# Gated linear attention with a convolved gate: one weight tile split without TensorE, the check counted earlier, the last store on ScalarE, a new order of all instructions

## The chip, the cores and the metric

The kernel runs on one core of one Trainium2 chip. The metric is the device time of one execution in microseconds; the time given for a kernel is the median of its runs.

## What is computed

The reference has two parts. The first is a linear attention with a forget gate for each channel, for 4 sequences of 768 tokens and 8 heads of 48 channels:

```python
f = 1.0 / (1.0 + np.exp(-f_logit))
for t in range(S):
    state = f[:, :, t, :, None] * state + np.einsum('bhd,bhe->bhde', k[:, :, t], v[:, :, t])
    y[:, :, t] = np.einsum('bhd,bhde->bhe', q[:, :, t], state)
```

The second part takes the heads side by side as `x` (768 x 384 for each sequence):

```python
h = np.maximum(x @ w_in, 0.0)                      # 384 -> 1024
conv_out[:, t] = sum over k of conv_w[k] * h[:, t + k - 1]
gate = 1.0 / (1.0 + np.exp(-conv_out))
return (h * gate @ w_out).astype(np.float32)       # 1024 -> 384
```

The three weights are 64-bit floats, read as pairs of 32-bit words.

## The kernel before

**Attention.** The loop runs over 24 steps: 4 sequences times 6 chunks of 128 tokens. For each step ScalarE makes the two gate factors `e` from the running sum of the gate's logarithms; VectorE multiplies them into the tile that holds k and q (L566, "the kq product"); TensorE makes the scores (L588), turns k over (L581), multiplies the masked scores with v (L608), updates the state (L616) and applies the state carried from before (L652). For the first nine steps the running sum is a matmul on TensorE (L551), for the rest a scan on VectorE (L558). ScalarE and VectorE copy the result as a rounded part and a rest into `xT` (L665, L667), and small transfers on SyncE's queue bring 16 rows of each into place (L675, "the gather").

**Gated product.** For half a sequence (384 tokens) and each of 8 blocks of 128 hidden units, the first product takes nine matmuls (L705: rounded and rest parts, three of the four combinations). ScalarE applies the relu (L715), ScalarE and VectorE the convolution (L721, L725), the gate (L729) and its product (L731). For each tile of 128 tokens the gated values are parted again into `gh` (L748, ScalarE) and `gl` (L752, VectorE); the second product is 16 matmuls with `gh` and 8 with `gl` (L761). The result is copied (L767) and stored (L771).

**Splitting the weights.** A 64-bit weight becomes a rounded float `hi` and a rest `lo`, in `split_f64`. There are seven tiles: three of `w_in` (1024 columns of `hi` each) and four of `w_out` (768). `CFG["ez"]` has a letter for each. Letter `d` takes four VectorE operations (mask L416, combine L419, mask L429, scale L444), one ScalarE copy (L435), and then "the join": for each half of the tile TensorE adds three products with a unit matrix in PSUM (L452 to L454) and ScalarE copies the sum out (L457). Letter `r` has no join: six VectorE operations (L414, L416, L419, L422, L425, L427) and one ScalarE copy (L424). Before, the letters are `dddrrrr`: all three tiles of `w_in` are joined on TensorE.

**The check at the end.** The fast path holds only for gates and weights inside a range. All `w_in` and `w_out` are read once more late in the program (L786 to L792) and a maximum kept for each piece; at the end VectorE turns these and the gates into a count (L803 to L805), one tiny matmul adds it up (L807), VectorE casts it (L808), every engine loads it into a register (L811), and a branch (L813) skips the slow path.

**The order.** `ORDER` is a list of all 1231 planned operations, and each engine and SyncE's queue take theirs in this order. A number with a point says which buffer of a ring is taken, a `v` that an operation which can run on ScalarE or VectorE runs on VectorE. Twelve of the operations are fillers, each a product of zeros (L381, `stir`, two matmuls in the records), that only keep TensorE busy. `LAST` names the one output tile whose store ScalarE issues instead of SyncE; before, it is tile 2 of the last sequence.

## Time and profile before

| | us |
|---|---|
| median of 3 runs | 303.0 (302.75, 303.0, 305.2) |
| the profiled execution's own time | 303.39 |
| its span, first to last instruction | 301.5 |
| TensorE busy (4319 matmuls) | 293.1 (97%) |
| VectorE busy | 255.3 (85%) |
| ScalarE busy | 241.8 (80%) |

The profiled execution is 0.4 us above the median, and 1.9 us of it lie outside the span. Matmuls are pipelined and overlap in the records, so a busy TensorE is not one at its peak; where it counts, the distance from the start of one instruction to the start of the next is read instead. VectorE's instructions, too, overlap the next one by a little under 0.1 us. Stretches differ: attention fills the first 220 us, the gated product begins at 42 us and is alone from 220 us on.

### The profile page before, as it was taken

The numbers are of one execution on the slowest core, as the hardware profiler recorded it, in microseconds if no ns is written. First come the engines' busy times: TensorE is split into PE (matmuls) and PEld (weight loads), VectorE is DVE, ScalarE is ACT, GpSimd is POOL, SyncE is SP. The second block draws the span as 40 slices with busy tenths as digits, with TensorE's granted clock in tenths as the row PEclk, the third lists the DMA queues.
The fourth block names the chain that finished last, engine by engine and source line by source line (L and its number), as shares of the span: only waits on it lengthen the run. The fifth ranks groups of instructions, "written<-read, shape, count | busy, mean of one in ns | idle before, by whom it ended". The sixth has DMA issues, their size and how long they took to land.

```text
span 301.5 us, 10053 instructions
## 1 busy us (share of the span) xinstructions
PE 293.1 (97%) x4319; PEld 276.4 (92%) x4319; DVE 255.3 (85%) x413; ACT 241.8 (80%) x482; POOL 2.8 (1%) x16
## 2 busy tenths in 40 slices
PE   8979999999999999999999999999999999999994
PEld 5767787998999999999999999999999999999993
DVE  3787999999999998999999997878985498499543
ACT  5677989999966899998979975876957797788541
POOL 3000000000000000000000000000000000000000
PEclk9999999999999999999999999999999999999998
DMA  6994998601460346622362444346040611313151
GB/s 211 395 362 138 332 331 306 183 2 30 130 253 0 99 145 218 187 74 72 102 215 60 167 164 121 101 137 201 21 145 14 191 51 47 96 54 97 71 175 58
DMA packets 19188, 43.38 MB, mean 144 GB/s; under 512 B 2732, under 2 KB 10052, under 8 KB 19140
## 3 DMA queue, kind: packets, MB, share of 16 engines
q1 hardware_dynamic: 18996, 42.50, 43.2%
q8 instruction: 35, 0.57, 0.8%
q10 hardware_dynamic: 144, 0.20, 0.2%
q14 instruction: 13, 0.11, 0.1%
HBM read 35.61 MB, written 4.72 MB: 134 GB/s over the span
## 4 chain that ended last, share of the span: by engine, by line
PE 88%; ACT 4%; DVE 3%; DMA 2%; issue 1%; SPq 0%; DVEq 0%; ACTq 0%
PE mm L761 33%; PE mm L705 33%; PE Y L608 4%; PE Y L616 4%; PE Y L652 4%; PE Y L581 3%; PE S L588 3%; DMA kq<-in_kq_dram 2%; PE mm L551 1%; PE mm L452 1%; DVE kq L566 1%; PE S L381 1%; ACT g L721 1%; ACT st L638 1%; ACT L729 0%
## 5 line engine op out<-in xcount | busy, mean ns | idle before, releaser
L705 PE MATMUL mm<-xT,wi 128*128 128x384 f32 x576 | 107.2, 340 | 0.1
L705 PEld LDWEIGHTS mm<-xT,wi 128*128 128x128 f32 x576 | 100.4, 188 | 1.1 <-ACT wi L457 0.2
L725 DVE SCALAR_TENSOR_TENSOR g<-hb,cw,g 128x384 f32<-128x384 f32 (+1 forms) x128 | 74.0, 614 | 8.1 <-ACT g L721 7.8
L761 PE MATMUL mm<-wo,gh 128*128 128x384 f32 x384 | 70.9, 337 | 0.0
L761 PEld LDWEIGHTS mm<-wo,gh 128*128 128x128 f32 x384 | 66.5, 188 | 0.3
L715 ACT ACTIVATE hb<-mm 128x384 f32<-128x384 f32 x64 | 31.3, 489 | 16.6 <-PE mm L705 16.2
L721 ACT ACTIVATE g<-hb,cw 128x384 f32<-128x384 f32 (+1 forms) x64 | 37.4, 613 | 2.2 <-DVE gl L752 2.1
L761 PE MATMUL mm<-wo,gl 128*128 128x384 f32 x192 | 37.1, 337 | 0.0
L752 DVE TENSOR_TENSOR gl<-g,gh 128x1024 fp32r<-128x1024 f32 (+2 forms) x28 | 29.5, 1067 | 8.1 <-ACT gh L748 7.1
L761 PEld LDWEIGHTS mm<-wo,gl 128*128 128x128 f32 x192 | 33.5, 188 | 0.1
L566 DVE TENSOR_TENSOR kq<-kq,e 128x1024 f32<-128x1024 f32 x24 | 29.1, 1214 | 4.6 <-DMA kq<-in_kq_dram 4.6
L731 DVE SCALAR_TENSOR_TENSOR g<-g,hb 128x768 f32<-128x768 f32 (+1 forms) x32 | 30.2, 956 | 3.0 <-ACT g L729 2.7
L748 ACT CAST gh<-g 128x1024 fp32r<-128x1024 f32 (+2 forms) x28 | 25.8, 933 | 7.8 <-PE mm L761 4.6
L729 ACT ACTIVATE g<-g 128x768 f32<-128x768 f32 (+1 forms) x32 | 26.5, 844 | 0.0
L608 PE MATMUL Y<-am,v 64*64 64x64 f32 (+1 forms) x768 | 24.0, 219 | 0.5 <-issue 0.5
L608 PEld LDWEIGHTS Y<-am,v 64*64 64x64 f32 (+1 forms) x768 | 19.0, 127 | 0.8 <-issue 0.8
L596 DVE COPY_PREDICATED am<-mask,S 128x512 f32<-128x512 uint8 x24 | 17.6, 734 | 1.8 <-PE S L588 1.8
L558 DVE TENSOR_TENSOR_SCAN fb<-runs,fb 128x512 f32<-128x512 f32 x15 | 18.0, 1214 | 0.0
L588 PE MATMUL S<-kq 48*64 48x64 f32 x768 | 16.8, 220 | 0.9 <-DVE kq L566 0.9
L667 DVE TENSOR_TENSOR xT<-Y,xT 112x512 fp32r<-112x512 f32 x24 | 16.3, 682 | 1.5 <-ACT xT L665 1.5
L616 PEld LDWEIGHTS Y<-v,kp 64*48 64x48 f32 (+1 forms) x704 | 13.7, 127 | 3.8 <-issue 2.7
L616 PE MATMUL Y<-v,kp 64*64 64x48 f32 (+1 forms) x704 | 16.2, 214 | 1.0 <-issue 1.0
(100 smaller groups left out, 349.5 us busy)
## 6 DMA issues: line engine op xcount, KB each, us to landing
kq<-in_kq_dram SPq DMA_DIRECT2D x24, 512.0 KB, 5.4
v<-in_v_dram SPq DMA_DIRECT2D x24, 192.0 KB, 4.4
out_dram<-ob SPq DMA_DIRECT2D x23, 192.0 KB, 2.2
fb<-in_f_logit_dram SPq DMA_DIRECT2D x15, 256.0 KB, 4.6
kq<-in_moe_w_in_dram SPq DMA_DIRECT2D x6, 512.0 KB, 4.1
kq<-in_moe_w_out_dram SPq DMA_DIRECT2D x6, 512.0 KB, 4.0
xT<-xT SPq DMA_DIRECT2D x48, 48.0 KB, 4.2
xT<-in_moe_w_in_dram SPq DMA_DIRECT2D x4, 512.0 KB, 7.2
```

The costliest lines, as they stand in the source:

```text
L566: ox = plan.op("DVE", 1222, lambda e, X=X, E=E: nc.vector.tensor_tensor(buf(X), buf(X), buf(E), ALU.mult), ka, need=[o2, ld_x], use=[X, E])
L588: o = nc.tensor.matmul(scores()[t, j, p, :], buf(X)[r, 0, p, t], buf(X)[r, 1, p, t], start=True, stop=True)
L608: o = nc.tensor.matmul(out_of(Y, p, j, w, z), buf(V).rearrange("p h d -> p (h d)")[t, h * D:h * D + w], buf(AM)[t, j, p, :], start=x == 1 ...
L616: nc.tensor.matmul(pk(z)[HP * j:HP * j + w, p, :], buf(KP)[t, p, HP * j:HP * j + w], buf(V)[t, 2 * p + j, :], start=True, stop=True)
L705: nc.tensor.matmul(buf(ph)[:, :HS], wi[:, t, wl, f * P:(f + 1) * P], x_view(pl, u)[:, t, xl, :], start=(i == 0), stop=(i == 3 * KT - 1))
L715: nc.scalar.activation(hb[:, 2:HS + 2], buf(ph)[:, :HS], AF.Relu, scale=0.5)
L721: o = pl.op("ACT", 620, lambda e, cv=cv, hb=hb, n=n, f=f: nc.scalar.activation(cv(), hb[:, 1:n + 1], AF.Copy, scale=cw[:, 1, f:f + 1]), ke ...
L725: o = pl.op("DVE", 617, lambda e, cv=cv, hb=hb, n=n, f=f, w=w, sh=sh: nc.vector.scalar_tensor_tensor(cv(), hb[:, sh:n + sh], cw[:, w, f:f ...
L729: o = pl.op("ACT", 846, lambda e, cv=cv: nc.scalar.activation(cv(), cv(), AF.Tanh), key, need=last, use=[("g", u)], mode="T")
L731: gates[u, fp] = pl.op("DVE", 960, lambda e, cv=cv, fp=fp, n=n: nc.vector.scalar_tensor_tensor(cv(), cv(), 1.0, h_b[:, fp:fp + 2, 1:n + 1] ...
L752: los.append(pl.op("DVE", 150 + 134 * nn * NF // 128, lambda e, hv=hv, lv=lv, src=src: nc.vector.tensor_tensor(lv(), src(), hv().bitcast(F ...
L761: nc.tensor.matmul(buf(po)[:, :DM], view(g)[:, f, :], wo[:, f, wl, :], start=(i == 0), stop=(i == 3 * NF - 1))
```

## The change

Four edits, and a new `ORDER` in which every operation has a new place.

1. The third letter of `ez` becomes `r`: one of the three `w_in` tiles is split without the join, so five of the seven tiles are.
2. The count is planned like any other operation and put before the `gl` part of the last tile; the copy of the last tile waits for it.
3. `LAST` is now the very last tile: its store is issued by ScalarE.
4. Two loads change shape: the gates of the last two groups of three steps come in one transfer of 768 KB each instead of three of 256 KB, and the kq tile of step 20 comes in two halves.

```diff
-           ... m2d=48.268, ez='dddrrrr')
+           ... m2d=48.268, ez='ddrrrrr')
 ORDER = """
-91.0 92 93 143.0 161.1 45.0 94 100.1 96 144.0 7.1 162.1 97.1 23.1 95.0 10.0 24 145.0 4.0 146.0 8.1 179.2 147 5.0 98
+89.0 43.0 90 137.0 91 138.0 92 23.1 93.0 24 44.0 8.1 98.1 94 155.1 6.0 156.1 1.0 9.1 139.0 2.0 140.0 7.1 95.0 173.2
...
-    LAST = (B - 1, CPH - 1)
+    LAST = (B - 1, NC - 1)
...
+        once = g >= len(groups) - 2 and not turned
-        for i in range(m):
-            n = first[g] + i
+        for i in range(0, m, m if once else 1):
+            n, k = first[g] + i, m if once else 1
...
-        ld_x = plan.op("SP", 430, lambda e, X=X, b=b, c=c: nc.sync.dma_start(buf(X), kq_in[b, c]), (n, "kq"),
-                       take=[("kq", X)], size=512)
+        ld_x = [plan.op("SP", 430, lambda e, X=X, b=b, c=c, z=z: nc.sync.dma_start(buf(X)[:, z], kq_in[b, c][:, z]), (n, "kq"),
+                        take=[] if z.start else [("kq", X)], use=[X] if z.start else [], size=512 // k)
+                for k in (2 if n == N - 4 else 1,) for z in (slice(y * 2 // k, (y + 1) * 2 // k) for y in range(k))]
...
-                    nc.scalar.copy if e == "ACT" else nc.vector.tensor_copy)(buf(ob), buf(po)[:, :DM]), key, need=[o],
+                    nc.scalar.copy if e == "ACT" else nc.vector.tensor_copy)(buf(ob), buf(po)[:, :DM]), key, need=[o] + (extra if (b, m) == (B - 1, NC - 1) else []),
...
+    def counting(e):
+        a = nc.vector.tensor_scalar(ok[:, :n_ft], ft_all.rearrange("p b c n -> p (b c n)"), F_MIN, None, ALU.is_ge)
+        nc.vector.tensor_scalar(ok[:, n_ft:], far, HALF * HALF, None, ALU.is_lt)
+        return a, nc.vector.tensor_reduce(oks, ok, mybir.AxisListType.X, ALU.add)
+
+    o = plan.op("DVE", 620, counting, N + 3.9, need=checks + keeps)
+    o = plan.op("PE", 60, lambda e: nc.tensor.matmul(one(), oks, ones, start=True, stop=True), N + 3.91, need=[o], take=[("S", "pn")],
+                mode="t", n=4)
+    counted = plan.op("DVE", 140, lambda e: nc.vector.tensor_copy(cnt_i, one()), N + 3.92, need=[o], use=["pn"])
+    moe(plan, gathered, [counted])
```

**The start of SyncE's queue.** The first transfers before; `fb` is a gate tile, `kq` and `v` are tiles of a step, `xT` is here the buffer into which raw weights are loaded.

```order
L514 DMA fb_111<-in_f_token_dram 128x384 x3
L540 DMA kq_113<-in_kq_dram 128x1024
L540 DMA kq_114<-in_kq_dram 128x1024
L464 DMA xT_144<-in_moe_conv_w_dram 24x256
L514 DMA fb_112<-in_f_token_dram 128x384
L542 DMA v_117<-in_v_dram 128x384
L542 DMA v_118<-in_v_dram 128x384
L464 DMA xT_153<-in_moe_w_in_dram 128x1024 x2
L540 DMA kq_115<-in_kq_dram 128x1024
```

The same place in the changed kernel.

```order
L515 DMA fb_111<-in_f_token_dram 128x384
L464 DMA xT_143<-in_moe_conv_w_dram 24x256
L515 DMA fb_111<-in_f_token_dram 128x384
L544 DMA kq_113<-in_kq_dram 128x1024
L515 DMA fb_111<-in_f_token_dram 128x384
L547 DMA v_117<-in_v_dram 128x384
L464 DMA xT_150<-in_moe_w_in_dram 128x1024 x2
L515 DMA fb_112<-in_f_token_dram 128x384
L544 DMA kq_114<-in_kq_dram 128x1024
```

The first weight tile has moved ahead of the second step's kq tile; 2328 KB are on the queue up to its end, where it was 3224 KB.

**VectorE ahead of the sixth kq product.** Before, the rows from the second `w_in` tile's second mask on; `gh`, `gl` and `ob` are here work tiles of a split, `am` the masked scores, `sh` and `st` the state.

```order
L429 TENSOR_SCALAR gl_487<-gh_385 128x1024
L444 SCALAR_TENSOR_TENSOR ob_507<-xT_262,gl_487 128x1024
L667 TENSOR_TENSOR xT_305<-Y_109,xT_305 112x4x128
L596 COPY_PREDICATED am_89<-mask_86,S 128x512
L692 MEMSET hb 128x2x2
L566 TENSOR_TENSOR kq_116<-kq_116,e_121 128x1024
L566 TENSOR_TENSOR kq_114<-kq_114,e_122 128x1024
```

In the changed kernel, from the last operation of the second tile on, which is the one split by letter `r`.

```order
L427 SCALAR_TENSOR_TENSOR wi<-gl_406,gh_375 128x2x512
L602 COPY_PREDICATED am_89<-mask_86,S 128x512
L414 TENSOR_SCALAR gl_522<-g_323 128x768
L673 TENSOR_TENSOR xT_321<-Y_109,xT_321 112x4x128
L572 TENSOR_TENSOR kq_116<-kq_116,e_122 128x1024
L416 TENSOR_SCALAR gh_562<-g_323 128x768
L635 TENSOR_TENSOR sh_96<-Y_110,st_94 112x192
L419 SCALAR_TENSOR_TENSOR gh_562<-g_323,gh_562 128x768
L422 SCALAR_TENSOR_TENSOR gl_522<-gl_522,g_323 128x768
L638 TENSOR_TENSOR st_93<-Y_110,sh_96 112x192
L602 COPY_PREDICATED am_90<-mask_86,S 128x512
L572 TENSOR_TENSOR kq_114<-kq_114,e_121 128x1024
```

The fifth and sixth kq products stood side by side; now four operations of a `w_out` tile, one masked copy and two of the state lie between them.

**The end of SyncE's queue.** Before: the last two stores, then the count's load (TENSOR_LOAD) and the branch.

```order
L771 DMA out_dram<-ob_4032 128x384
L771 DMA out_dram<-ob_4079 128x384
L811 TENSOR_LOAD cnt_i
L811 ISA x2
L813 COMPARE_AND_BRANCH
```

Now:

```order
L777 DMA out_dram<-ob_4037 128x384
L822 TENSOR_LOAD cnt_i
L822 ISA x2
L777 DMA out_dram<-ob_4079 128x384
L824 COMPARE_AND_BRANCH
```

The count's load has moved ahead of the last store but one, and the last store (tile `ob_4083`) has left this queue for ScalarE's.

## Rows read from the trace of the kernel before

**Rows 1.** Busy time by stretch: PE, PEld, DVE, ACT, POOL, then PEclk, DMA share, GB/s.

```profile
8.44:32.66 24.22, 21.69 (x483) 17.12 (x482) 20.33 (x34) 18.17 (x46) 0.00 (x0) 1.00 0.84 305
32.66:42.28 9.62, 9.62 (x243) 7.72 (x244) 9.62 (x18) 8.78 (x25) 0.00 (x0) 1.00 0.97 310
42.28:72.00 29.72, 29.65 (x598) 26.93 (x598) 29.46 (x49) 29.25 (x61) 0.00 (x0) 1.00 0.48 161
72.00:130.00 58.00, 58.00 (x818) 56.13 (x820) 56.68 (x87) 51.54 (x95) 0.00 (x0) 1.00 0.43 138
130.00:220.00 90.00, 89.67 (x1730) 86.23 (x1718) 82.05 (x135) 74.97 (x158) 0.00 (x0) 1.00 0.39 122
220.00:297.20 77.20, 77.20 (x448) 76.91 (x443) 53.84 (x84) 54.22 (x95) 0.00 (x0) 1.00 0.30 93
```

**Rows 2.** The chain that ended last, in order of time: start, length, what.

```profile
11.89 0.43 PE S L381 x2
...
42.28 3.15 PE mm L705 x18
...
272.19 24.97 PE mm L761 x144
297.19 0.56 DVE ob L767
```

**Rows 3.** Timeline of TensorE, two joins and what follows them: start, length, instruction.

```profile
48.06 1.13 PE L452 MATMUL mm<-gh,ident 128*128 128x512 f32 x2
...
50.81 0.60 PE L581 MATMUL Y<-ident,kq 128*128 128x128 f32 x4
```

**Rows 4.** Groups by line, shapes apart: the split's operations; busy us, mean ns.

```profile
L457 ACT CAST wi<-mm 128x512 fp32r<-128x512 f32 x6 | 3.5, 604 | 0.0
...
L419 DVE SCALAR_TENSOR_TENSOR gh<-xT,gh 128x1024 int32<-128x1024 int32 x2 | 2.4, 1217 | 0.0
L444 DVE SCALAR_TENSOR_TENSOR ob<-xT,gl 128x1024 fp32r<-128x1024 uint32 x2 | 2.4, 1215 | 0.0
...
L416 DVE TENSOR_SCALAR gh<-xT 128x1024 int32<-128x1024 int32 x2 | 1.4, 679 | 0.0
```

**Rows 5.** Timeline, the first 20 us: first weight load, first kq product, first split.

```profile
5.88 1.30 SPq L464 DMA_DIRECT2D xT<-in_moe_w_in_dram  x2
...
8.44 1.23 DVE L566 TENSOR_TENSOR kq<-kq,e 128x1024 f32<-128x1024 f32 x1 [4.61 <-DMA kq<-in_kq_dram]
...
14.76 0.68 DVE L416 TENSOR_SCALAR gh<-xT 128x1024 int32<-128x1024 int32 x1
```

**Rows 6.** Timeline, 31 to 47 us: kq products five and six, sixth score, last scale.

```profile
31.53 2.35 DVE L566 TENSOR_TENSOR kq<-kq,e 128x1024 f32<-128x1024 f32 x2
...
39.38 0.68 PE L588 MATMUL S<-kq 48*64 48x64 f32 x32
...
45.52 1.21 DVE L444 SCALAR_TENSOR_TENSOR ob<-g,gl 128x1024 fp32r<-128x1024 uint32 x1
```

**Rows 7.** Timeline, the first tile of the second product, around 95 us.

```profile
94.90 1.28 DVE L752 TENSOR_TENSOR gl<-g,gh 128x1016 fp32r<-128x1016 f32 x2
...
97.27 1.03 PE L761 MATMUL mm<-wo,gl 128*128 128x384 f32 x5
```

**Rows 8.** Waits of TensorE's weight loads between 32.7 and 297 us: total, times, longest.

```profile
PEld Y L652 <- issue: 2.1, 10, 0.4
```

**Rows 9.** Lines L771, L811, L813, L979: ns min/median/max, first and last start.

```profile
297.77 0.34 SPq L771 DMA_DIRECT2D out_dram<-ob  x1
...
DMA to landing us min/median/max: 1.8/1.9/3.4
...
L811 SPq TENSOR_LOAD <-cnt_i x1: 539/539/539, 298.2 to 298.2; - x1
...
L813 SPq EVENT_SEMAPHORE  x8: 17/17/17, 299.6 to 300.2; - x8
...
L979 SPq EVENT_SEMAPHORE  x10: 17/28/28, 300.2 to 301.5; - x10
```

## The prediction

> **What bounds the kernel now.** I read the busy time by stretch first, because the share over the whole run mixes stages with different limits. From 32.66 us on TensorE is busy all the time, in every stretch up to 297.2 us [rows 1]. Ahead of that it is not: between 8.44 and 32.66 us TensorE lacks 2.5 us, VectorE 3.9 and ScalarE 6.1 of 24.22 us. The second thing in these rows is that TensorE is not alone. VectorE is full from 32.66 to 42.28 us, lacks 0.3 of 29.72 us after that and 1.3 of 58 us up to 130 us; only from 130 us on does it have room (82.05 of 90 us, then 53.84 of 77.2). ScalarE is full from 42 to 72 us.

> The chain that ended last comes next [rows 2]. Its last long piece is the second product, 24.97 us from 272.19 us on without a gap, and after it only the copy of the last tile. So a microsecond of TensorE's work that is taken out is a microsecond off the end, provided the other two engines can keep up where they are full as well. That proviso is the whole question here.

> **What the change takes from TensorE.** One tile of three loses its join, that is two join halves. Two of them stand side by side at 48 us [rows 3]: from the start of the first to the start of what follows is 50.81 - 48.06 = 2.75 us. Counted with the order: four halves stood ahead of the first product before and two do now, and two stand behind it in both. So 2.75 us go, all from the part ahead of 42.28 us, where the first product starts [rows 2]. One filler moves from the start to behind the last product: 0.43 us more [rows 2], between nothing (it stood in a gap) and 0.43; I take 0.4. Behind the last product it runs while the last tile is copied and stored.

> The new order changes how often TensorE goes over from one kind of work to another: 99 changes after against 94 before, counted in the order over products, scores, small attention matmuls and turns. No row shows the price of one change; the nearest is the wait of "issue" ahead of the carried-state matmuls, 2.1 us in ten [rows 8], 0.2 each. Five more cost between nothing and 1.0 us; I take 0.3, since that wait is only one of the kinds, and three more of the changes went away with the joins.

> **What it adds to VectorE.** On tiles of 1024 a mask takes 0.68 us and a combining or scaling operation 1.22 [rows 4]. Letter `d` has two of each, 3.8 us; letter `r` has three of each, 5.7 us. VectorE gets 1.9 us more. ScalarE loses the two copies of the join, 2 x 0.60 = 1.2 us [rows 4].

> The sixth kq product is the place to test it, because the sixth score stands behind it and the first product behind that. Ahead of it VectorE's list is now longer by the 1.9 us, by the first four operations of a `w_out` tile (two masks and two others on 768 columns, three quarters of the sum above, 2.8 us), and by a masked copy and a few short state operations (about 1.2): 5.9 us in all. Before, the sixth kq product began at 32.7 us (the second of the two, [rows 6]), and the score that needs it at 39.38 [rows 6]. So there were 39.38 - 33.88 = 5.5 us of slack. If VectorE keeps all its 3.9 us of idle time, the product ends at 33.9 + 5.9 = 39.8 us, and the score can start 0.4 us later than it did. If it gives all of it back, it ends at 35.9 us, and TensorE, 3.2 us earlier at 36.2 us, does not wait.

> Does the idle time go? Most of it lay between the first kq product at 8.44 and the first split at 14.76 us [rows 5], where VectorE waited for scores and had no weights to work on. The transfers come in the order of SyncE's queue, and the first weight tile now ends 2328 instead of 3224 KB down the queue. At 305 GB/s, the mean of that stretch [rows 1], 0.9 MB are 2.9 us. The second kq tile comes later by about as much, but VectorE has the split to do in that time. I take it that 2.5 us or more come back, which is what the first product needs to start 3 us earlier.

> Behind that, VectorE's work up to the tiles of the second product is nearly what it was: the `w_out` operations that came earlier are missing later, and three copies of k that VectorE made stand on ScalarE now. The first tile of the second product is the tightest place: its `gl` is ready at 96.2 us and used at 97.27 [rows 7], so TensorE may come 1.1 us sooner for nothing, and for the rest VectorE must be earlier too, by the same regained time.

> **What it changes at the end.** Before, the last copy starts at 297.19 us [rows 2], SyncE issues the store at 297.77 and then loads the count (0.54 us from 298.2), branches, and goes through eight waits from 299.6 to 300.2 us [rows 9]. By the median of its line the store has landed at 297.77 + 1.9 = 299.7 us. So SyncE's own path, not the store, set the end. Now the count is loaded ahead of the last store but one, and ScalarE issues the last store. SyncE then has only to wait for it; SyncE's transfers take eight semaphores in turn, and in the new order this one is the eighth, the last to be waited for. It ends at 299.7 instead of 300.2: 0.5 us, between nothing (ScalarE issues later, the landing takes up to 3.4) and 0.5. I take 0.4. The count itself costs TensorE a tiny matmul that it had before.

> The 768 KB gate transfers and the halved kq tile cost nothing in my sum: they serve steps for which VectorE has room (after 130 us), and the kq half only lets the wait start sooner. If a buffer came free late for a whole group, the group's first step would wait; the rows give no price for that, and I leave it to the range.

> **The sum.** 303.39 - 2.75 - 0.4 + 0.3 - 0.4 = 300.1 us for the profiled execution. The median was 303.0, 0.4 us below that execution, so 299.7 us. A measurement of this kernel can tell about 1% from no change, that is 3.0 us; the forecast lies just at that edge.

> **The rivals.** *VectorE keeps its idle time.* Then the sixth score starts at 39.8 instead of 39.38 us, the join halves and the filler that no longer stand ahead of it give TensorE nothing but waiting, and only the tail is left: 303.0 + 0.4 - 0.4 = 303.0 us. For it speaks that the second kq tile now stands behind 1.4 MB more on the queue; against it, the weights that come sooner.

> *VectorE sets the pace from 42 to 130 us.* It lacks only 1.6 of 87.7 us there [rows 1]; the 1.9 us of the new letter then go onto the end, with 0.4 back at the tail: 304.5 us. Against it stands that the work up to the second product is nearly the same in sum. [...]

> *Slower: the third `w_in` tile comes late.* The order keeps its join on TensorE right behind the first two blocks of the first product, and its second half is loaded only behind the first gather. Before, the last scale ended at 46.73 us [rows 6] and the join began at 48.06. Everything on TensorE stands behind this join, so each microsecond by which the scale ends after 46.8 us is one at the end. It must end 3.5 us later, at 50.3 us, for the whole to be 1% slower; at 51 us the time would be 303.0 + 4.2 - 0.4 = 306.8 us. VectorE's list up to there is only 0.5 us longer, which speaks against it.

> *More than forecast.* If the regained time on VectorE also removes the waits of TensorE ahead of 32.66 us, up to 2.5 us [rows 1], 1.8 of them would give 297.9 us.

> **Chances.** Forecast 0.58 (its own range 298.4 to 301.2), more 0.10, idle time kept 0.16, VectorE's pace 0.10, slower 0.06. Of the forecast's share three fifths lie below 300.0 us, 0.35; with the better case 0.45 for faster by over 1%. The rest of it with the two cases near 303 us makes 0.49 within 1%; slower is 0.06. The range goes from 297.8 to 303.2 us: it leaves out the slower case, most of the case of VectorE's pace and a little at the lower end.

> **What would show it.** Right: four join halves instead of six; the first product begins at 39 to 40 us; VectorE busy for more than 22 us between the first kq product and 32.7 us, with its first split at about 12 us; no wait of TensorE at the first tile of the second product; from the last matmul to the end 3.9 us instead of 4.3. Wrong: a first product at 42 us (idle time kept), waits of TensorE for `gl` or for a relu between 42 and 130 us (VectorE's pace), or a join that waits for its scale (the late tile).

## The result, and the profile after

The changed kernel takes 305.19 us (median of 21 runs, 304.4 to 310.9), the kernel before, run beside it on the same chip, 303.11 us (median of 21, 301.99 to 305.2). The ratio is 1.0067 with a 95% interval of 1.0047 to 1.0087: slower by 0.7%. The forecast was 299.7 us with a range of 297.8 to 303.2; the time lies outside it, on the other side of no change. The run of 310.9 us belongs to a slower state (mean granted clock 0.989), and the ratio leaves such runs out. The profiled execution of the changed kernel took 304.6 us with a span of 302.8; before, these were 303.39 and 301.5.

The busy time by stretch of the changed kernel (columns as in [rows 1], which are the same stretches of before):

```profile
8.44:32.66 24.22, 20.57 (x476) 16.04 (x475) 21.48 (x39) 19.09 (x50) 0.00 (x0) 1.00 0.83 314
32.66:42.28 9.62, 8.30 (x243) 7.40 (x243) 9.48 (x15) 8.17 (x22) 0.00 (x0) 1.00 0.75 223
42.28:72.00 29.72, 29.27 (x565) 26.52 (x564) 27.97 (x46) 28.33 (x56) 0.00 (x0) 1.00 0.59 199
72.00:130.00 58.00, 58.00 (x812) 56.02 (x811) 57.30 (x88) 50.46 (x97) 0.00 (x0) 1.00 0.41 124
130.00:220.00 90.00, 90.00 (x1718) 86.02 (x1720) 80.56 (x129) 78.64 (x170) 0.00 (x0) 1.00 0.41 128
220.00:297.20 77.20, 77.20 (x487) 76.67 (x482) 54.11 (x85) 53.37 (x94) 0.00 (x0) 1.00 0.27 87
```

From 42.28 us to the end of the second product TensorE is as full as before: 0.4 us less up to 72 us, 0.3 more from 130 to 220 us. The difference in idle time lies ahead of it: in the first two stretches TensorE is without work for 24.22 - 20.57 + 9.62 - 8.30 = 4.97 us, where it was 2.53 [rows 1]. That is 2.44 us more, and the joins that went are worth nearly as much (2.75). This is a timeline of TensorE at the third `w_in` tile's join, which stayed:

```profile
48.71 1.13 PE L452 MATMUL mm<-gh,ident 128*128 128x512 f32 x2
...
50.13 1.02 PE L452 MATMUL mm<-gh,ident 128*128 128x512 f32 x2
...
51.45 0.60 PE L587 MATMUL Y<-ident,kq 128*128 128x128 f32 x4
```

From 48.71 to 51.45 us it takes 2.74 us, as it did [rows 3], and there is one such pair fewer ahead of it. The chain that ended last (start, length, what) says where the gain stood afterwards:

```profile
42.22 3.19 PE mm L711 x18
...
272.86 22.19 PE mm L767 x128
...
298.22 0.56 DVE ob L773
```

The first product starts at 42.22 us, where it was 42.28 [rows 2]: nothing is left of the 2.75 us. The last copy starts at 298.22 us, where it was 297.19 [rows 2], so another 1.09 us were lost behind the start of the first product. Such places are those of one execution each: `e8` below has the same instructions up to the end, and its first product starts at 41.09 us.

What TensorE waited for, 0 to 66 us (what waited and for whom, us in total, times, longest), first before, then in the changed kernel:

```profile
PE mm L381 <- DVE stir L308: 1.2, 1, 1.2
PE Y L616 <- issue: 1.0, 1, 1.0
PE S L588 <- DVE kq L566: 0.9, 2, 0.5
PE S L381 <- DVE am L596: 0.3, 1, 0.3
PE mm L452 <- ACT wi L457: 0.3, 1, 0.3
PE Y L608 <- issue: 0.2, 1, 0.2
```

```profile
PE Y L614 <- issue: 1.8, 2, 1.4
PE mm L381 <- DVE stir L308: 1.2, 1, 1.2
PE Y L622 <- ACT kp L598: 1.0, 1, 1.0
PE mm L556 <- ACT e L567: 0.9, 2, 0.7
PE mm L556 <- issue: 0.6, 1, 0.6
PE Y L658 <- DVE st L638: 0.6, 1, 0.6
PE Y L622 <- issue: 0.3, 1, 0.3
```

The waits for ScalarE and VectorE changed their names (kq, am and wi before, kp, e and st after) and grew by about 1 us, from 1.5 to 2.5. The larger part is the one without a name: "issue", a wait in which nothing that the profile shows held the engine, grew from 1.2 to 2.7 us. The timeline shows the odd thing about it: three of the four places (TensorE's matmuls, in brackets the idle time before them).

```profile
30.59 0.34 PE L614 MATMUL Y<-am,v 64*48 64x64 f32 x8 [1.36 <-issue]
...
41.17 1.05 PE L556 MATMUL mm<-tri,fg 128*128 128x128 f32 x7 [0.62 <-issue]
...
47.68 0.37 PE L614 MATMUL Y<-am,v 64*64 64x64 f32 x10 [0.44 <-issue]
```

Each stands in the middle of matmuls of one line, with the same inputs as the matmul before it. I counted TensorE's instructions in the traces of all kernels here: weight loads, matmuls and the semaphore instructions between them, the first as number 0. Up to 66 us the stops of matmuls without a name (over 0.15 us) come at the 449th, 705th, 961st, 1217th, 1473rd and 1729th, and at no other; behind that the kernel before has one at the 4801st (0.33 us, at 137.45 us) and the changed kernel none. All are multiples of 256 apart. And of the queue that the profile calls "q8 instruction" one packet of 16 KB ends 1.2 to 1.6 us ahead of the stop's end, each time. This is its row of the DMA view of the changed kernel from 0 to 50 us:

```profile
q8 instruction: 6, 0.10, 0.8%
```

When each piece began, and in brackets how long TensorE had stood still for it (us; the last two rows are experiments, below):

```
piece's first instruction   449th        705th        961st        1217th   1473rd       1729th
before                      18.00 (0.96) 24.40 (0.17) 29.01        37.04    40.40        46.87
changed                     19.33        24.37 (0.29) 30.59 (1.36) 36.70    41.17 (0.62) 47.68 (0.44)
changed, thin weights       20.14        24.89        30.01 (0.27) 36.12    40.67 (0.69) 46.46
before, thin weights        19.91        26.17        30.81        38.83    42.20        48.64
```

Why there: these are the rates of the DMA engines in 40 slices from 14 to 35 us, before and after.

```profile
GB/s 424 387 412 432 366 383 389 407 404 358 408 381 399 416 328 103 70 35 0 0 0 31 0 140 133 421 311 145 243 240 331 360 395 386 372 363 391 380 365 363
```

```profile
GB/s 429 421 398 387 396 284 59 137 213 351 384 382 383 307 357 412 359 390 386 414 369 410 420 439 401 429 402 354 120 29 0 0 0 0 31 0 0 82 82 102
```

Before, the engines are nearly empty from 22 to 26 us (0 to 103 GB/s), and the packet of the 961st starts at 25.5 us. In the changed kernel they are full from 19 to 28.5 us (307 to 439 GB/s), and the same packet starts at 28.2. In both, TensorE had come to the piece before at 24.4 us. Up to 48 us in the two traces a piece's packet starts 0 to 4.2 us after TensorE has come to the piece before; behind that, where the engines move less [rows 1], from 3.2 us ahead of it to 2.9 us after it.

### The profile page after: what moved, and what is told of

Same layout as the page of the kernel before. It is cut to its first block, busy times and chain, and to the rows that moved or that the text cites. A ratio compares the mean times of both kernels' runs of the same rounds, so it can differ in the third digit from the quotient of the medians.

```text
span 302.8 us, 10039 instructions
## 1 busy us (share of the span) xinstructions
PE 291.9 (96%) x4311; PEld 274.7 (91%) x4311; DVE 254.2 (84%) x410; ACT 241.9 (80%) x489; POOL 2.8 (1%) x16
## 4 chain that ended last, share of the span: by engine, by line
PE 92%; DVE 3%; issue 2%; ACT 2%; DVEq 0%
PE mm L711 34%; PE mm L767 34%; PE S L594 4%; PE Y L614 4%; PE Y L658 4%; PE Y L622 3%; PE Y L587 3%; PE mm L381 2%; PE mm L556 2%; PE mm L452 1%; DVE kq L572 1%; DVE gh L419 1%; PE S L381 0%; ACT e L565 0%; DVE gh L416 0%
## 5 line engine op out<-in xcount | busy, mean ns | idle before, releaser
L711 PE MATMUL mm<-xT,wi 128*128 128x384 f32 x576 | 108.8, 341 | 0.0
L614 PE MATMUL Y<-am,v 64*48 64x64 f32 (+1 forms) x768 | 24.0, 220 | 1.8 <-issue 1.8
L644 ACT ACTIVATE st<-st,ft_all 112x48 f32<-112x48 f32 x72 | 18.1, 325 | 3.4 <-DVE st L638 3.3
L598 ACT COPY kp<-Y 128x512 f32<-128x512 f32 x24 | 13.9, 580 | 4.7 <-PE Y L587 4.6
L773 ACT COPY ob<-mm 128x384 f32<-128x384 f32 x22 | 10.3, 468 | 9.1 <-PE mm L767 9.0
```

What stands on the lines that cost most here:

```text
L614: o = nc.tensor.matmul(out_of(Y, p, j, w, z), buf(V).rearrange("p h d -> p (h d)")[t, h * D:h * D + w], buf(AM)[t, j, p, :], start=x == 1 ...
L711: nc.tensor.matmul(buf(ph)[:, :HS], wi[:, t, wl, f * P:(f + 1) * P], x_view(pl, u)[:, t, xl, :], start=(i == 0), stop=(i == 3 * KT - 1))
```

## The experiments

Two theories. F: the late pieces, behind the weight transfers, took the gain of the joins. The rival: VectorE's longer list, or the waits for ScalarE, hold TensorE, and a late piece only shows a wait that would come elsewhere.

**The letter alone, in the old order.** The third letter changes; on VectorE's list the two operations that it adds and three of a `w_out` tile get new places, the rest stays as before. `e6` spreads these operations differently over the list.

```diff
-           ... ez='dddrrrr')
+           ... ez='ddrrrrr')
...
```

> The kernel before with the letter r for the third tile and nothing else: its two join halves and their copies leave the old order, its two added VectorE operations stand behind the sixth kq product, the first three operations of the first w_out tile behind the masked copy that followed them. Theory A (the removed joins are worth their time; the new order gave it back in waits of TensorE ahead of 52 us): the two join halves are 2.75 us of TensorE, up to 1 us is lost to waits, 300.4 to 301.5 us beside 303.1. Rival B (VectorE sets the pace up to 130 us, so its 1.9 us more go onto the end): 303.1 to 305.0 us.

> The kernel before with the letter r once more, VectorE's list laid out with care: the fifth kq product ahead of the sixth, then the tile's two late operations, masked copy and state, and only behind them the w_out tile, whose second half stands behind the third w_in tile's. Theory A (the time of e1 came of its list: TensorE waited 1.7 and 2.9 us for VectorE where the joins had been, and the granted clock fell behind it): first product at 40.5 to 41.5 us, clock 1.0 throughout, 301.3 to 302.5 us beside 303.1. Rival B (VectorE's 1.9 us set the first product whatever the list): first product at 42.3 us or later, 303.0 to 305.0 us.

305.84 us, 1.0080 [1.0059, 1.0102], and 306.51, 1.0116 [1.0069, 1.0162]: slower both times, and above the ranges of both theories. In the profiled execution of `e1` (308.0 us, the longest of its eight) TensorE waits for VectorE (idle time in brackets), and the granted clock (the first of the last three columns of the second view) is then about half of full speed, 0.52:

```profile
33.91 0.66 PE L581 MATMUL Y<-ident,kq 128*128 128x128 f32 x4 [1.65 <-DVE kq L566]
...
40.28 0.70 PE L652 MATMUL Y<-kq,sh 48*48 48x64 f32 x16 [2.87 <-DVE st L632]
```

```profile
39.50:46.50 7.00, 6.22 (x141) 6.10 (x141) 6.97 (x11) 4.24 (x11) 0.00 (x0) 0.52 0.93 306
```

In `e6` the longest such wait is 2.6 us, and the granted clock is 1.00 around it. So in neither list did VectorE take the letter's 1.9 us without TensorE waiting for it; a new order was needed for the letter, as far as these two lists show.

**The letter back, in the new order.** The other half of that question: the old letter in the changed kernel, its two join halves put among the attention matmuls (the order's lines are left out here).

```diff
-           ... ez='ddrrrrr')
+           ... ez='dddrrrr')
...
```

> The changed kernel with the letter d for the third tile again: its two join halves stand in the new order behind the two running sums that follow the fourth score and the fifth turn, two VectorE operations go (1.9 us), the other five keep their places. Theory A (the removed work stood beside waits of TensorE ahead of the first product, so that taking it out bought little): the two halves cost less than 1 us, 304.3 to 306.0 us beside 305.2. Rival (in the new order TensorE's work there counts in full): 305.2 + 2.75 us, 307.2 to 308.3 us.

308.06 us, 1.0157 [1.0119, 1.0195]. So in the new order the letter gains 308.06 - 305.19 = 2.9 us, near the 2.75 of the sum (the two intervals leave more than 1 us either way); and the order with the other edits costs 308.06 - 303.11 = 5.0 us. (The place of the joins is my choice, the waits of "issue" in its profiled execution are 0.9, 1.4 and 1.5 us, and the granted clock falls there, to 0.58 from 44 to 46 us and 0.57 from 46 to 48, so neither is an exact price.)

**The last store.** ScalarE issues the last store in the old kernel (`e7`); SyncE issues it in the new one (`e8`).

```diff
-    LAST = (B - 1, CPH - 1)
+    LAST = (B - 1, NC - 1)
```

> The kernel before with the last store issued by ScalarE and nothing else. By the step of the prediction (SyncE's own path set the end, so its relief is worth 0.3 to 0.5 us): 302.6 to 302.8 us beside 303.1. Theory C (the store issued by ScalarE lands later and is the last to be waited for): 303.1 to 303.9 us.

> The changed kernel with the last store issued by SyncE again and nothing else (the store of the tile that LAST named before goes to ScalarE). Theory C (landing of the ScalarE store, 2.6 us in the profiled execution where SyncE's take 1.9, sets the end): 304.4 to 304.8 us beside 305.2. By the step of the prediction SyncE is late again: 305.2 to 305.7 us.

303.45 us, 0.9993 [0.9965, 1.0022], and 304.86 us, 1.0051 [1.0029, 1.0073]: no effect that these runs can tell in either kernel.

**The sixth kq product earlier.** VectorE's list of the changed kernel with the sixth kq product ahead of three operations of a `w_out` tile.

```diff
-L416 TENSOR_SCALAR gh<-g 128x768
-L419 SCALAR_TENSOR_TENSOR gh<-g,gh 128x768
-L422 SCALAR_TENSOR_TENSOR gl<-gl,g 128x768
 L638 TENSOR_TENSOR st<-Y,sh 112x192
 L572 TENSOR_TENSOR kq<-kq,e 128x1024
+L416 TENSOR_SCALAR gh<-g 128x768
+L419 SCALAR_TENSOR_TENSOR gh<-g,gh 128x768
+L422 SCALAR_TENSOR_TENSOR gl<-gl,g 128x768
```

> The changed kernel with the sixth kq product, and the state operations and the masked copy that go with it, ahead of three operations of the w_out tile on VectorE. Theory A1 (VectorE's longer list ahead of the sixth kq product is what holds the first product at 42.2 us): the product starts at 41.0 to 41.6 us and the time is 304.0 to 304.6 us beside 305.2. Rival A2 (TensorE's waits ahead of it, those without a releaser above all, hold it): 305.0 to 305.4 us.

306.1 us, 1.0095 [1.0069, 1.0121]. The wait for VectorE is gone, one of 1.0 us for ScalarE's copy of a join (L457) has come, the first product still starts at 41.88 us (A1 expected 41.0 to 41.6), and the piece of the 1729th stops TensorE for 2.36 us, after which the granted clock falls to 0.53:

```profile
49.61 0.37 PE L614 MATMUL Y<-am,v 64*64 64x64 f32 x10 [2.36 <-issue]
```

```profile
50.50:53.50 3.00, 3.00 (x17) 1.69 (x10) 3.00 (x6) 2.40 (x4) 0.00 (x0) 0.53 0.93 338
```

So VectorE's list alone is not what holds it.

**Weight transfers moved.** (F's expectations are called A2 in `e3`.) `e3` moves the first half of the third `w_in` tile three transfers back; `e13` puts both halves side by side ahead of the gathers; `e11` does the opposite in the kernel before, and loads both halves and a piece of `w_out` sooner, into its gap at 22 to 26 us.

```diff
-L464 DMA xT<-in_moe_w_in_dram 128x1024
 L547 DMA v<-in_v_dram 128x384
-L681 DMA xT<-xT 16x768 x2
 L544 DMA kq<-in_kq_dram 128x1024
-L681 DMA xT<-xT 16x768 x4
-L464 DMA xT<-in_moe_w_in_dram 128x1024
+L464 DMA xT<-in_moe_w_in_dram 128x1024 x2
+L681 DMA xT<-xT 16x768 x6
```

(the diff of `e13`, SyncE's queue)

> The changed kernel with one transfer moved: the first half of the third w_in tile (512 KB, issued at 22.6 us) behind the second gather transfer (33 us). Theory A2 (the wait of 1.36 us in the middle of a run of matmuls at 29.2 us is TensorE's next block of instructions, which comes by the same DMA engines and stands behind the outstanding transfers): the wait shrinks to 0.6 us or less, the gathers are issued 0.7 to 1.3 us sooner and the time is 304.0 to 304.8 us beside 305.2. Rival: the wait does not hang on the transfers, stays at 1.2 to 1.5 us, and the time is 305.0 to 305.4 us.

> The changed kernel with three transfers moved on SyncE's queue: the seventh kq tile and behind it both halves of the third w_in tile stand ahead of the six gather transfers, where the queue had nothing outstanding from 29 to 33 us, instead of one half at 22.6 us ahead of the fetch and the rest at 34 to 37 us. Theory F (late blocks of instructions gave the gain back): waits without a releaser at 29 us 0.6 us or less, at 41 us 0.2 us or less, at 47 us 0.4 us or less; first product at 40.6 to 41.4 us and 303.6 to 304.4 us beside 305.2. Rival (the waits move on, or others take their place): 305.0 to 305.5 us.

> The kernel before with three weight transfers (1.4 MB: the second piece of w_out and both halves of the third w_in tile) moved ahead of the fifth kq tile's on SyncE's queue, into the gap that the queue had from 18 to 25 us. Theory F: the fetch that came at 25.5 us comes 2 us or more later, a wait without a releaser of 0.5 to 1.7 us appears at 29 us where there was none, and the time is 303.6 to 304.8 us beside 303.1. Rival (weights that come sooner can only help, TensorE's instructions do not wait for them): 302.6 to 303.2 us.

`e3`: the stop at the 961st shrank from 1.36 to 0.55 us, as F has it, and the one at the 1473rd grew from 0.62 to 1.72: 305.19 us, 1.0069 [1.0039, 1.0099], nothing gained. `e13`: stops of 0.82 and 1.14 us, none at the 1473rd: 304.77 us, 1.0053 [1.0017, 1.0088], above F's 303.6 to 304.4 and under the rival's 305.0. `e11`: against its edge the packet started only 1.3 us later than before, and came in time, and 303.44 us is 0.9989 [0.9959, 1.0020]: F expected a loss, so this one went the rival's way. Where a stop was relieved here, TensorE reached a later edge sooner and waited longer there: in `e3` from 39.77 us on at the 1473rd, in `e13` from 46.40 on at the 1729th, where it had been 40.55 and 47.24.

**The start.** ScalarE's two gate factors of the first step stand side by side again, without a logarithm between them (`e14`; an earlier trial let the score read k and q ahead of the kq product and tells nothing); `e15` adds `e13` and SyncE's last store, `e16` also `e2`.

```diff
 L565 ACTIVATE e<-mm 128x512
+L567 ACTIVATE e<-mm 128x512
 L534 ACTIVATE fg<-fb 128x8x48
-L567 ACTIVATE e<-mm 128x512
```

> The changed kernel with another start, the score behind its kq product: ScalarE makes both gate factors of the first step before the logarithm of the second, TensorE has the filler ahead of the second running sum and the first score ahead of the first turn. Theory A3 (the late start counts): first score at 10.1 to 10.6 us instead of 11.3 and 304.2 to 304.8 us beside 305.2. Rival (the lead is lost at the second kq product, which waits for its place on VectorE's list): 305.0 to 305.5 us.

> e13 and e14 together, the last store on SyncE as in e8. Theory F and A3: first product at 40.0 to 41.0 us, 302.4 to 303.8 us. Rival: 304.7 us or more.

> e15 with VectorE's list of e2 (the sixth kq product ahead of three operations of the w_out tile). If VectorE's list is late once the other waits are gone: first product 0.5 to 1.0 us sooner than in e15 and 0.4 us or more off its time. If not: within 0.3 us of e15.

`e14`: the first score comes 0.88 us sooner (10.39 us instead of 11.27), and the stops at the 705th, 961st and 1729th grow to 0.99, 1.64 and 1.40 us, while that at the 1473rd goes: 305.04 us, 1.0045 [1.0024, 1.0066]. `e15`: 304.74 us, 1.0037 [1.0004, 1.0070]. `e16`: stops of 1.09, 1.43, 0.29 and 2.38 us, 306.02 us, 1.0076 [1.0054, 1.0098]. None beats the kernel before, and `e3`, `e14` and `e15` came out at the times of their rivals: by the time alone the moves do not speak for F.

**Gate transfers moved.** Loads of the gates at 38 to 44 us put behind weights (`e9`), with `e3` (`e10`), or with `e2` and SyncE's store (`e12`).

```diff
-L517 DMA fb_112<-in_f_logit_dram 128x512 x3
+L517 DMA fb_111<-in_f_logit_dram 128x512 x3
 L464 DMA g_323<-in_moe_w_out_dram 128x768 x2
-L517 DMA fb_111<-in_f_logit_dram 128x512 x3
...
+L517 DMA fb_112<-in_f_logit_dram 128x512 x3
```

> The changed kernel with the gates of steps 9 to 11 loaded and worked on ahead of those of steps 12 to 14 instead of behind them, and the 768 KB of the latter loaded behind the last four w_out pieces (about 50 us instead of 38 to 40). Theory F (TensorE's next 256 instructions come by the DMA engines and stand behind what is outstanding there; where the fetch is late TensorE waits, and after a long wait the granted clock falls): the wait at 47.2 us (0.4 us in the profiled execution of the changed kernel, 1.7 in that of e8, with 3.4 us at half clock behind it) goes to 0.2 us or less, no stretch at half clock before 72 us, 304.3 to 304.8 us beside 305.2 and none of the runs above 306. Rival (those waits do not hang on the transfers): 305.0 to 305.4 us with the same spread.

> The changed kernel with the transfers of e9, VectorE's list of e2 and the last store on SyncE as in e8. Theory F with A1 and C: first product at 41.3 to 41.9 us, no half clock before 72 us, 303.4 to 304.4 us. Rival: the waits only move on, 305 us or more.

313.9, 314.33 and 314.35 us. My list brought the gates so late that TensorE stood 6.5 us (`e9`) behind ScalarE's relu at 60 us. That swamps what they were for, and they tell nothing of F.

**The bytes taken away.** Two last runs keep every instruction and its order, and shorten the weights' transfers themselves, in both kernels. Three quarters of each weight tile are not loaded but set to zero by GpSimd, which is added work; with most weights zero these two kernels do not compute the reference.

```diff
-        return plan.op("SP", 430, lambda e: nc.sync.dma_start(plan.buf(i)[:r, at:at + n], src), key,
+        m = n // 4 if nbytes > 24 else n
+        def load(e):
+            if m < n:
+                nc.gpsimd.memset(plan.buf(i)[:r, at + m:at + n], 0)
+            return nc.sync.dma_start(plan.buf(i)[:r, at:at + m], src[:, :m])
+        return plan.op("SP", 430, load, key,
```

> The changed kernel, with each tile of w_in and w_out loaded in its first quarter of columns alone; the other three quarters of the raw tile are set to zero by GpSimd (so three quarters of the weights are zero here). Every other instruction and its order are those of the changed kernel, and some 4.6 MB less cross the DMA engines in the first 45 us. Theory F (the fetches of TensorE's next 256 instructions queue behind the weight transfers, and the waits at these edges gave the 2.75 us of the joins back): the waits of TensorE that nothing releases, 0.29, 1.36, 0.62 and 0.44 us at 24.1, 29.2, 40.6 and 47.2 us in the changed kernel, shrink to 0.3 us or less in all ahead of 52 us; the first product starts at 39.5 to 41 us instead of 42.2; the time is 301.5 to 303. Rival (VectorE's list and the waits for ScalarE hold TensorE, and an edge only shows a wait that would come elsewhere): the waits at the edges go, and as much comes back as waits for VectorE, ScalarE or a load; the first product stays at 42 us or later and the time at 304.5 or more.

> The kernel before, with the same three quarters of each tile of w_in and w_out left out of the load and set to zero by GpSimd. Theory F: the edges cost the kernel before little in the first 52 us (0.96 and 0.17 us at 17.0 and 24.2 us), so it gains 1 us or less by it: 302 to 303, and it is slower than the changed kernel with thin weights by 0.5 us or more, where it is 2 us faster with whole ones. Rival: the changed kernel stays slower than the kernel before by 1 us or more with thin weights too, since what holds it isn't the transfers.

The changed kernel: 302.9 us, 0.9984 [0.9966, 1.0003] of the kernel before with whole weights; up to 50 us 10.75 MB cross its data queue instead of 14.01, that is 3.3 MB less, not the 4.6 expected. The kernel before: 303.9 us, 1.0016 [0.9993, 1.0039]. What TensorE waited for in the changed kernel with thin weights (lines are 7 further down):

```profile
PE mm L381 <- DVE stir L308: 1.2, 1, 1.2
PE Y L629 <- ACT kp L605: 1.0, 1, 1.0
PE mm L563 <- ACT e L574: 0.9, 2, 0.7
PE mm L563 <- issue: 0.7, 1, 0.7
PE Y L665 <- DVE st L645: 0.6, 1, 0.6
PE Y L621 <- issue: 0.3, 1, 0.3
```

Against the view of the changed kernel above, the waits for kp, e and st are what they were, and nothing took their place; "issue" fell from 2.7 to 1.0 us; the stop at the 1473rd stayed, at 0.69 us, against F's 0.3 or less. The median fell by 305.19 - 302.9 = 2.3 us. That is F's forecast (301.5 to 303) and not the rival's (304.5 or more). About 0.4 us of it may lie in the clock: the five longest of the changed kernel's 21 runs with whole weights (306.5 to 310.9 us) have a mean granted clock of 0.994 or less, the other sixteen, with 0.996 or more, a median of 304.8, and none of its runs with thin weights is under 0.997. Its first kq product in the timeline, and its first product in the chain:

```profile
10.11 1.22 DVE L579 TENSOR_TENSOR kq<-kq,e 128x1024 f32<-128x1024 f32 x1 [2.55 <-ACT e L574]
```

```profile
41.71 3.15 PE mm L718 x18
```

The first product, at 41.71 us, lies outside F's 39.5 to 41. But the first kq product starts 0.82 us later than with whole weights (9.29 us, below). That is the clock, not the weights: it rose to full at 7.41 us in this execution and at 5.78 in the other (two pairs of filler matmuls start 0.85 us apart here, at 5.85 and 6.70 us, and 0.44 there, at 5.81 and 6.25), and TensorE's first running sum starts at 7.49 instead of 6.68 us; in `e13`, with whole weights and the clock up at 7.43 us, it starts at 7.49 us too. Take the 0.82 off, and the first product comes at 40.9 us. The kernel before lost more at the start: beside GpSimd's clearing, which runs to 9.5 us there, a cast of VectorE (L316, from 2.25 us on) takes 7.34 us instead of 1.23, its first score waits 2.0 us for VectorE instead of 0.3, and then the granted clock is half of full speed, in the same column as above:

```profile
PE S L595 <- DVE kq L573: 2.8, 2, 2.0
```

```profile
12.00:13.00 1.00, 1.00 (x5) 1.00 (x6) 0.95 (x3) 0.00 (x0) 0.00 (x0) 0.50 1.04 370
```

That covers the 1.1 us of "issue" that it was rid of. So its 303.9 us lie outside my expectation (302 to 303), and the intervals of the two overlap. Five of its twelve runs, 304.3 to 305.3 us, have a mean granted clock of 0.992 or 0.993; the other seven have a median of 302.94, the time of the changed kernel. What is shown is the fall of the changed kernel; that it would beat the kernel before with thin weights is not.

## Why the prediction was wrong

*The joins.* Right: four halves, and 2.74 us for the pair that stayed. With the old letter in the new order the kernel is 2.9 us slower.

*The step that failed* is "I take it that 2.5 us or more come back, which is what the first product needs to start 3 us earlier", and with it the whole account by VectorE's slack. These are the rows that answer to [rows 5, 6], with the first score (11.27 us):

```profile
3.67 0.91 SPq L464 DMA_DIRECT2D xT<-in_moe_w_in_dram  x2
...
9.29 1.23 DVE L572 TENSOR_TENSOR kq<-kq,e 128x1024 f32<-128x1024 f32 x1 [5.47 <-ACT e L567]
...
11.27 0.69 PE L594 MATMUL S<-kq 48*64 48x64 f32 x32
...
12.66 0.68 DVE L416 TENSOR_SCALAR gh<-xT 128x1024 int32<-128x1024 int32 x1
...
36.95 1.21 DVE L572 TENSOR_TENSOR kq<-kq,e 128x1024 f32<-128x1024 f32 x1
...
38.22 0.69 PE L594 MATMUL S<-kq 48*64 48x64 f32 x32
```

The first split comes 2.1 us sooner, at 12.66 us, as foreseen; the first kq product comes 0.85 us later, at 9.29 us, because TensorE's first running sum starts at 6.68 us instead of 5.71, and ScalarE's second gate factor now stands behind a logarithm of the next step (0.4 us). A turn now stands ahead of the first score as well, and the score comes 1.55 us later than before, when it was

```profile
9.72 0.69 PE L588 MATMUL S<-kq 48*64 48x64 f32 x32 [0.33 <-DVE kq L566]
```

So from the first score to the first product it is 42.22 - 11.27 = 30.95 us, and was 42.28 - 9.72 = 32.56: 1.6 us did come back there, and as much had been lost ahead of it. `e14` gave back 0.88 of that, and its median did not follow. VectorE is idle for 2.7 us from 8.44 to 32.66 us instead of 3.9: 1.2 us back, not 2.5. The sixth kq product ends at 36.95 + 1.21 = 38.2 us, between the 35.9 and 39.8 of the forecast. Its score starts right behind it, 1.2 us sooner than before [rows 6], and had waited for it for 0.26 us at most (the idle time of TensorE's weight loads there): so VectorE, which I had watched, held TensorE little here. TensorE had come late by itself. So the removed time did not become an earlier first product. The sum took it that the time of removed instructions goes over to the start of the next; it had no term for TensorE's own supply of instructions. [rows 1] hold the hint: with 305 and 310 GB/s the DMA engines were busy for 0.84 and 0.97 of these stretches, and I used that to time the weights, not to ask what else crosses the same engines.

From 8.44 to 42.28 us the waits of TensorE grew by 2.44 us: 1.14 at the edges (0.29 + 1.36 + 0.62 against 0.96 + 0.17), 1.06 in the waits for kp, e and st, the rest in gaps below 0.2 us. Behind it the idle time grew by 0.05 us in all (0.44 at the edge at 47.68 us, against 0.33 that went between 130 and 220 us), so about 1.0 of the 1.09 us lies in TensorE's busy time; its cause stays open. The thin weights turn this account into a shown one for the edges: 1.7 us of "issue" and 2.3 us of the median go with the transfers, and the other waits do not change. That is as much as the kernel lost against the one before (2.08 us), and less than half of the 5.5 us between forecast and time. Why it is not 3 us faster even with thin weights stays open: the later first score, the 1.06 us of waits and the busy time behind 42 us were not parted. What the waits for ScalarE cost by themselves stays open: `e14` took 0.5 us of the wait for e away, and the edges took it up.

*The filler and the changes of kind* (-0.4 and +0.3): the filler went, as said. From joins, filler and waits alone the first product should start 2.75 + 0.43 - 2.44 = 0.74 us sooner; it starts 0.06 sooner. The 0.68 us left hold the changes of kind and the work that changed its place; I did not part them.

*The tail* (-0.4): wrong, +0.3. From the copy's start to the end of the span it was 301.5 - 297.19 = 4.3 us and is now 302.8 - 298.22 = 4.6; the filler there runs beside the copy. The count is early, as planned (SyncE loads it at 295.4 us), but the store is later and slower (issue and landing, us from issue):

```profile
298.81 0.38 ACTq L777 DMA_DIRECT2D out_dram<-ob  x1
```

```profile
out_dram<-ob ACTq DMA_DIRECT2D x1, 192.0 KB, 2.6
```

It lands at 298.81 + 2.6 = 301.4 us, 3.2 us behind the copy's start; [rows 9] had 2.5. SyncE's wait for it is the last of its waits to end, at 301.4 us: so the end went from SyncE's path to the store. The 1.9 us of the median landing was the wrong figure, the row's own maximum of 3.4 was the bound to mind. It is not a matter of the issuing engine: in `e7` ScalarE's last store landed in 1.9 us, and in `e8` SyncE's wait for its own last store ended 2.7 us after its issue. Why the last store takes longer in the new order stays open. `e7` and `e8` bear out that nothing is to be had.

*The rivals.* The measured time is nearest to the 304.5 us of "VectorE sets the pace", and by another way: TensorE is full from 72 to 130 us and waits for no `gl`, and VectorE's 57.30 of 58 us cost nothing there. In `e1` and `e6`, in the old order, TensorE does wait long for VectorE, up to 2.87 and 2.60 us; in the changed kernel no wait for it behind the first 2 us is longer than 0.6 us (for st, ended at 36.47 us). "VectorE keeps its idle time" had the right sign of a first product at 42 us, which the prediction named as the sign against it, and the wrong cause. The third tile's join waited for no scale. No rival had a wait that takes the joins' place on TensorE itself.

## What to carry to other kernels

A tuned order can be tuned to waits that no line of code shows: here the 256 instructions of TensorE from the 961st on came in where the DMA engines had a gap, at 25.5 us. Before counting removed instructions as gained time, look in the trace for stops that nothing releases, and count the instructions between them, the short ones and waits on semaphores included. Where the counts are equal, as the multiples of 256 on TensorE were here, ask what the DMA engines carry while the engine runs through the piece before the stop. A wait of "issue" in the middle of a run of equal instructions was the sign here; moving one transfer moved it to a later edge, and only fewer bytes took most of it away (2.7 to 1.0 us). And look at the first score too: an order that takes work out later but begins 1.55 us later has not gained yet.

## What was not expected of the hardware

In these traces TensorE's instructions compete with data: stops of up to 2.38 us (`e16`), up to 66 us always at the same six counts, each with a packet of 16 KB that ends 1.2 to 1.6 us ahead of the stop's end; and with 3.3 MB less on the data queue the waits of "issue" fell from 2.7 to 1.0 us. And the granted clock: in the profiles of before and after it is full from 6 us to the end of the product, but where TensorE had stood still for 2.36 us (`e2`) or was in a wait of 2.87 us with 1.65 us of another shortly before (`e1`), it was at half of full speed for 3.4 and 6.8 us (0.53 and 0.52 in the stretches above), and for 3.4 us after the first score's 2.0 us in the kernel before with thin weights (0.50). It also fell after stops of 1.52 (`e5`, 0.57 from 46 to 48 us) and 1.67 us (`e8`, 0.50 from 50 to 52 us), and after waits of 2.60 us (`e6`) and 1.72 us (`e3`) it stayed at 1.00, so the length of one wait does not tell. So 3.4 to 6.8 us at half clock can follow a wait here, beyond its own length, and need not; the longest runs of the changed kernel, up to 310.9 us, fit this, with mean granted clocks of 0.994 and 0.989, but no trace of them shows where it fell.
